# The first key chunk of an adaLN + linear attention + SwiGLU kernel: finer loads, ScalarE normalises, matvecs between the key matmuls

## The chip, the cores and the metric

The kernel runs on one core of a Trainium2 chip. The metric is the device time of one execution in microseconds (us). A profile's span starts at the first instruction, so it is 1.7 to 2.2 us shorter than the time in the runs here.

Engines in the profile: PE is TensorE (matmul), PEld its weight load, DVE is VectorE, ACT is ScalarE, POOL is GpSimd, SPq the queue that issues loads. The granted clock (PEclk) is the share of its full rate that TensorE's clock was given. A matvec is a matmul of a weight block with one column. To modulate a tile is to multiply by `1 + ca` and add `sa`; `xn` is a normalised tile, `tp` its transpose as TensorE writes it, `hT` the copy of `tp` that the matmuls read.

## The reference, cut to what matters

```python
x = A_x                                               # 2048 x 1024, bf16
mod = (silu(c) @ w_mod).reshape(1, 6, 1, -1)          # sa, ca, ga, sb, cb, gb
h = layernorm(x) * (1 + ca) + sa
qkv = h @ wqkv                                        # then linear attention with phi(q), phi(k)
x = x + ga * (attention(qkv) @ wo)
h = layernorm(x) * (1 + cb) + sb
x = x + gb * ((silu(h @ w_gate) * (h @ w_up)) @ w_down)
```

This is about the first 34 us: `layernorm` of the first 512 rows, the modulation vectors `ca` and `sa`, and the first 64 matmuls of `h @ wqkv` for the keys.

## The kernel before

The rows are worked on in four chunks of 512, each of four tiles of 128. In the first chunk everything has to arrive at once. Cut to the opening:

```python
for st in range(STC - 1):                  # three x tiles first; c was issued before them
    load_x(st, nc.sync)
for b in range(2):
    for q in (1, 0):                       # ca block, then sa block, 1 MB each
        t = big("wme", [DC, NB])
        nc.sync.dma_start(out=t[:], in_=wm_v[:, :, q * D + b * NB:...])
    for i in range(2):                     # two key rows of 128 x 1024 in one load
        nc.sync.dma_start(out=wk[b][:, 2 * i:2 * i + 2, :], in_=...)
    if b == 0:
        load_x(STC - 1, nc.sync)
# ... cut ...
def pe_transpose_tile(hT, xn, t):
    tp = acc_b("tp", (DC, P), BF16)
    for cc in range(DC):
        transpose(tp[:, cc, :], xn[:, cc * P:(cc + 1) * P])
    h = DC // 2
    nc.scalar.copy(out=hT[:, 0:h, ...], in_=tp[:, 0:h, :])
    nc.vector.tensor_copy(out=hT[:, h:DC, ...], in_=tp[:, h:DC, :])
# ... cut ...
keep_warm(accs[5], 26)                     # warmers: matmuls whose result is not used
with in_order(nc.vector, nc.scalar, nc.gpsimd):
    st0 = ln1_stats(0, 0)
    st1 = ln1_stats(0, 1)
    xn0 = ln1_norm(*st0)                   # VectorE normalises in chunk 0
    st2 = ln1_stats(0, 2)
    xn1 = ln1_norm(*st1)
    pe_transpose_tile(hTs[0], xn0, 0)
    xn2 = ln1_norm(*st2)
    keep_warm(accs[5], 4)                  # and 4 after tile 1 and after tile 2
    # ... cut ...
    for b in range(2):
        mod_block(b, 1); keep_warm(idle, 2)    # 32 matvecs for ca
        mod_block(b, 0); keep_warm(idle, 3)    # 32 matvecs for sa
        for cc in range(4 * b, 4 * b + 4):
            modulate(hTs[0], cc, ca1T, saT, 0, 3 * P)
        if b == 0:
            xn3 = ln1_norm(*ln1_stats(0, 3))
            k_mms(0, gs, accs, 0, 4)       # 24 key matmuls
            pe_transpose_tile(hTs[0], xn3, 3)
        else:
            k_mms(0, gs, accs, 4, 8)       # 24 more
    # ... cut: modulate tile 3, the last 16 key matmuls, evacuation
build_masks()                              # GpSimd memsets, needed much later
```

`ln1_stats` takes mean and variance on VectorE (`mv`) and the reciprocal root `rstd` on GpSimd. When ScalarE normalises, GpSimd must also compute `nmr = -mean * rstd`. `in_order` pins the traced order of instructions on VectorE, ScalarE and GpSimd; the scheduler may still put other instructions between them.

Of the kernel before, what the change touches and what calls it, by code (L numbers as in the profile page):

```python
# [8 lines left out]
ACT = mybir.ActivationFunctionType  # L9
# [12 lines left out]
def kernel(  # L22
# [13 lines left out]
    nc = tc.nc  # L36
    P = nc.NUM_PARTITIONS
    _, S, D = A_x.shape
# [4 lines left out]
    DC = D // P  # L43
    HG = DC
    FC = F // P
    SCW = 512
    NSC = S // SCW
    STC = SCW // P
    NB = 512
# [11 lines left out]
    wqkv_v = A_wqkv.rearrange("(c p) n -> p c n", p=P)  # L61
# [4 lines left out]
    wm_v = w_mod.rearrange("(p j) n -> p j n", j=DC)  # L66
    c_v = c.rearrange("o (p j) -> p (o j)", j=DC)
# [12 lines left out]
    last_on = {}  # L80

    @contextmanager
    def in_order(*engines):
        types = [e.engine for e in engines]
        traced = nc.cur_bb.bb.instructions
        mark = traced[-1]
        yield
        first = next(k for k in reversed(range(len(traced))) if traced[k] is mark) + 1
        for i in traced[first:]:
            if i.engine in types:  # L90
                prev = last_on.get(i.engine)
                if prev is not None:
                    tc.add_manual_dep(i, prev.name, mybir.DependencyInfo(
                        mybir.DependencyClass.NoSync, mybir.DependencyReason.DATA), reason="in_order")
                last_on[i.engine] = i

    def mm(out, lhsT, rhs, start, stop):
        return tc.keep_in_program_order(nc.tensor.matmul(out, lhsT=lhsT, rhs=rhs, start=start, stop=stop))  # L98

    def transpose(out, in_):  # L100
        return tc.keep_in_program_order(nc.tensor.transpose(out, in_, ident[:]))  # L101

    def big(name, shape):
        return k8.tile([P] + shape, BF16, name=name, tag="k8")
# [4 lines left out]
    def acc_b(name, shape=(NB,), dt=F32):  # L109
        return pb.tile([P] + list(shape), dt, name=name, tag="pb")  # L110
# [1 line left out]
    x1_dram = dram.tile([S, D], F32, name="x1_scratch")  # L112

    c_sb = const.tile([P, DC], BF16, name="c_sb")
    nc.sync.dma_start(out=c_sb[:], in_=c_v)

    x_tiles = {}

    def load_x(st, eng):
        x_sb = k2.tile([P, D], BF16, name="x_sb")  # L120
        eng.dma_start(out=x_sb[:], in_=x2[st * P:(st + 1) * P, :])
        x_tiles[st] = x_sb

    for st in range(STC - 1):
        load_x(st, nc.sync)

    wme = []
    wk = [big("wk", [4, D]), big("wk", [4, D])]
    for b in range(2):
        ts = []  # L130
        for q in (1, 0):
            t = big("wme", [DC, NB])
            nc.sync.dma_start(out=t[:], in_=wm_v[:, :, q * D + b * NB:q * D + (b + 1) * NB])
            ts.append(t)
        wme.append(ts)
        for i in range(2):
            nc.sync.dma_start(out=wk[b][:, 2 * i:2 * i + 2, :], in_=wqkv_v[:, 4 * b + 2 * i:4 * b + 2 * i + 2, D:2 * D])
        if b == 0:
            load_x(STC - 1, nc.sync)

    def load_w(view, lo, name):
        ts = []
# [14 lines left out]
    nc.vector.memset(neg_half[:], -0.5)  # L157

    scT = const.tile([P, DC], BF16, name="scT")
    nc.scalar.activation(out=scT[:], in_=c_sb[:], func=ACT.Silu)  # L160
    sc32 = const.tile([P, DC, 32], BF16, name="sc32")

    saT = const.tile([P, DC], F32, name="saT")
    ca1T = const.tile([P, DC], F32, name="ca1T")
# [37 lines left out]
    def normalise(dst, src, mean, rstd):  # L202
        nc.vector.tensor_scalar(out=dst, in0=src, scalar1=mean, scalar2=rstd, op0=ALU.subtract, op1=ALU.mult)

    def normalise_act(dst, src, mv, rstd):
        nmr = small.tile([P, 1], F32, name="nmr")
        nc.gpsimd.tensor_scalar(out=nmr[:], in0=mv[:, 0, 0:1], scalar1=rstd[:, 0:1], scalar2=-1.0,  # L207
                                op0=ALU.mult, op1=ALU.mult)
        nc.scalar.activation(out=dst, in_=src, func=ACT.Identity, bias=nmr[:], scale=rstd[:, 0:1])  # L209

    def modulate(hT, cc, scaleT, biasT, lo=0, hi=SCW):
        nc.vector.tensor_scalar(out=hT[:, cc, lo:hi], in0=hT[:, cc, lo:hi], scalar1=scaleT[:, cc:cc + 1],  # L212
                                scalar2=biasT[:, cc:cc + 1], op0=ALU.mult, op1=ALU.add)

    def pe_transpose_tile(hT, xn, t):
        tp = acc_b("tp", (DC, P), BF16)
        for cc in range(DC):
            transpose(tp[:, cc, :], xn[:, cc * P:(cc + 1) * P])
        h = DC // 2
        nc.scalar.copy(out=hT[:, 0:h, t * P:(t + 1) * P], in_=tp[:, 0:h, :])  # L220
        nc.vector.tensor_copy(out=hT[:, h:DC, t * P:(t + 1) * P], in_=tp[:, h:DC, :])

    hTs = {}

    def ln1_stats(sc, t):
        x_sb = x_tiles.pop(sc * STC + t)
        mv = small.tile([P, STC, 2], F32, name="mv")
        bn(x_sb, mv[:, 0, :])
        rstd = rstd_of(mv, 1)
        return sc, t, x_sb, mv, rstd  # L230

    def ln1_norm(sc, t, x_sb, mv, rstd):
        xn = k2.tile([P, D], BF16, name="xn", bufs=4)
        if sc == 0:
            normalise(xn[:], x_sb[:], mv[:, 0, 0:1], rstd[:, 0:1])
            return xn
        normalise_act(xn[:], x_sb[:], mv, rstd)
        nc.sync.dma_start_transpose(hTs[sc][:, :, t * P:(t + 1) * P], xn[:])

    def ln1(sc):  # L240
        hTs[sc] = big("hT", [DC, SCW])
        for t in range(STC):
            ln1_norm(*ln1_stats(sc, t))

    def mod_block(b, q):
        k = 1 - q
        for i in range(4):
            col = q * DC + 4 * b + i
            for j in range(DC):
                mm(mod_ps[:, col:col + 1], lhsT=wme[b][k][:, j, i * P:(i + 1) * P],  # L250
                   rhs=scT[:, j:j + 1], start=(j == 0), stop=(j == DC - 1))
        cs = slice(4 * b, 4 * b + 4)
        src = mod_ps[:, q * DC + 4 * b:q * DC + 4 * b + 4]
        if q == 1:
            nc.vector.tensor_scalar_add(out=ca1T[:, cs], in0=src, scalar1=1.0)
        else:
            nc.vector.tensor_copy(out=saT[:, cs], in_=src)
# [12 lines left out]
    k_groups = [(t, nb) for t in range(STC) for nb in range(NNB)]  # L270

    def k_mms(sc, gs, accs, cc_lo=0, cc_hi=DC):
        for cc in range(cc_lo, cc_hi):
            for (t, nb), acc in zip(gs, accs):
                mm(acc[:], lhsT=hTs[sc][:, cc, t * P:(t + 1) * P], rhs=wk[cc // 4][:, cc % 4, nb * NB:(nb + 1) * NB],
                   start=(cc == 0), stop=(cc == DC - 1))

    def k_evac(sc, gs, accs):
        for (t, nb), acc in zip(gs, accs):
            phi_to(pks[sc][:, t, nb * NB:(nb + 1) * NB], acc[:])  # L280
# [118 lines left out]
    def keep_warm(acc, n):  # L399
        for _ in range(n):  # L400
            mm(acc[:], lhsT=sel[:, 0, :], rhs=sel[:], start=True, stop=True)

    gs = k_groups[0:6]
    accs = [acc_a() if i < 4 else acc_b("acc") for i in range(6)]
    keep_warm(accs[5], 26)
    hTs[0] = big("hT", [DC, SCW])
    pks[0] = big("pk", [STC, D])
    with in_order(nc.vector, nc.scalar, nc.gpsimd):
        st0 = ln1_stats(0, 0)
        st1 = ln1_stats(0, 1)  # L410
        xn0 = ln1_norm(*st0)
        st2 = ln1_stats(0, 2)
        xn1 = ln1_norm(*st1)
        pe_transpose_tile(hTs[0], xn0, 0)
        xn2 = ln1_norm(*st2)
        keep_warm(accs[5], 4)
        pe_transpose_tile(hTs[0], xn1, 1)
        keep_warm(accs[5], 4)
        pe_transpose_tile(hTs[0], xn2, 2)
        keep_warm(accs[5], 4)  # L420
        mod_ps = acc_b("mod_ps")
        for b in range(2):
            idle = accs[5] if b == 0 else accs2[0]
            mod_block(b, 1)
            keep_warm(idle, 2)
            mod_block(b, 0)
            keep_warm(idle, 3)
            for cc in range(4 * b, 4 * b + 4):
                modulate(hTs[0], cc, ca1T, saT, 0, 3 * P)
            if b == 0:  # L430
                xn3 = ln1_norm(*ln1_stats(0, 3))
                k_mms(0, gs, accs, 0, 4)
                pe_transpose_tile(hTs[0], xn3, 3)
                accs2 = [acc_b("acc")]
            else:
                k_mms(0, gs, accs, 4, 8)
        for cc in range(DC):
            modulate(hTs[0], cc, ca1T, saT, 3 * P, SCW)
        gs2 = k_groups[6:8]
        accs2.append(acc_b("acc"))  # L440
        k_mms(0, gs2, accs2)
        k_evac(0, gs, accs)
        k_evac(0, gs2, accs2)
    nc.vector.tensor_copy(out=sc32[:], in_=scT[:].unsqueeze(2).to_broadcast([P, DC, 32]))
    build_masks()

    for sc in range(NSC):
# [204 lines left out]
```

## Time and profile before

| | before |
|---|---|
| time, median of the runs beside the changed kernel | 847.84 us |
| TensorE busy share of the span | 99% |
| tile 0 normalised, tile 2 normalised | 7.93 us, 12.07 us |
| first key matmul | 16.30 us |
| first value matmul (all 64 key matmuls done) | 33.92 us |

The first question is where time can be won at all. The page gives the busy time of each engine and the share of each engine in the chain of work that ended last (before):

```profile
PE 838.6 (99%) x4284; PEld 385.7 (46%) x4284; DVE 307.2 (36%) x602; ACT 173.8 (21%) x267; POOL 55.7 (7%) x160
...
PE 98%; DVE 1%; POOL 0%; DMA 0%; issue 0%; ACT 0%; SPq 0%; DVEq 0%; POOLq 0%
```

The kernel is bound by TensorE. What the opening can gain is only the moment from which TensorE runs densely. The timeline of PE (before; start, length, what, count) shows that moment:

```profile
1.21 7.20 PE L98 MATMUL acc<-sel 128*128 128x512 bf16 x26 [1.21 <-DVE sel L397]
8.25 0.61 PE L101 MATMUL tp<-ident,xn 128*128 128x128 bf16 x8
...
12.13 0.62 PE L101 MATMUL tp<-ident,xn 128*128 128x128 bf16 x8 [0.49 <-DVE xn L203]
...
16.30 5.35 PE L98 MATMUL acc<-wk,hT 128*128 128x512 bf16 x24
...
25.27 8.81 PE L98 MATMUL acc<-wk,hT 128*128 128x512 bf16 x40
33.92 13.98 PE L98 MATMUL acc<-wv,hT 128*128 128x512 bf16 x64
```

The warmers (`acc<-sel`) run from 1.21 us (0.43 us apart until 4.15, then 0.21), the transposes of tile 2 at 12.13, the first key matmuls at 16.30, and from 25.27 on there is no gap. Of the 33.92 us, 64 key matmuls at 0.217 us are 13.9 us.

### The profile page before, as it was taken

Reading aid. Unit: us, or ns where it says so; the run is one execution under the profiler, and the core shown is the slowest. Engines: PE = TensorE matmul, PEld = TensorE weight load, DVE = VectorE, ACT = ScalarE, POOL = GpSimd, SP = SyncE. Lnnn points to the kernel's source line nnn. Section 1 sums busy time; section 2 is a strip of 40 time slices with the busy share of each in tenths; the row PEclk is TensorE's granted clock in tenths of the full one; section 3 lists DMA queues with packets and bytes.
Section 4 is the critical chain, followed back from the end, with each engine's and each line's share of the span. In section 5 each row is a group of like instructions: output and inputs, shape, how many; then the busy total and the mean of one; then the engine's idle time right before and its main releaser. Section 6 shows DMA issues by size and latency. Waiting matters only on the chain.

```text
span 846.2 us, 10498 instructions
## 1 busy us (share of the span) xinstructions
PE 838.6 (99%) x4284; PEld 385.7 (46%) x4284; DVE 307.2 (36%) x602; ACT 173.8 (21%) x267; POOL 55.7 (7%) x160
## 2 busy tenths in 40 slices
PE   8999999999999999999999999999999999999997
PEld 4445445544444444444444444444444444444443
DVE  5756464467423325431111344211114431111121
ACT  1455453354311110101111010011110101111000
POOL 2101010012011001100000010000001100000000
PEclk9999999999999999999999999999999999999999
DMA  9893870029976765528434073581604639710011
GB/s 309 301 257 98 243 187 1 1 52 215 348 210 207 214 186 174 181 69 266 146 104 149 19 236 95 159 283 54 199 1 126 185 69 318 240 59 0 19 57 50
DMA packets 125840, 128.74 MB, mean 152 GB/s; under 512 B 33376, under 2 KB 107360, under 8 KB 125280
## 3 DMA queue, kind: packets, MB, share of 16 engines
q1 hardware_dynamic: 122208, 115.36, 46.0%
q0 software_dynamic: 3584, 12.72, 5.0%
q8 instruction: 33, 0.54, 0.3%
q14 instruction: 15, 0.12, 0.0%
HBM read 108.01 MB, written 12.71 MB: 143 GB/s over the span
## 4 chain that ended last, share of the span: by engine, by line
PE 98%; DVE 1%; POOL 0%; DMA 0%; issue 0%; ACT 0%; SPq 0%; DVEq 0%; POOLq 0%
PE acc L98 88%; PE a_ps L98 7%; PE kvp L98 1%; PE modr L98 0%; PE wf L98 0%; DMA x_sb<-in_A_x_dram 0%; DVE stats L199 0%; PE mod_ps L98 0%; PE den L98 0%; POOL zmask L186 0%; PE tp L101 0%; POOL rstd L193 0%; PE bcr L98 0%; DVE e L583 0%; DVE ob L585 0%
## 5 line engine op out<-in xcount | busy, mean ns | idle before, releaser
L98 PE MATMUL acc<-h2T,wgu 128*128 128x512 bf16 x1792 | 387.9, 379 | 0.0
L98 PEld LDWEIGHTS <-wgu 128*128 128x128 bf16 x1792 | 175.1, 98 | 211.0
L98 PE MATMUL acc<-wd,gu 128*128 128x512 bf16 x896 | 196.0, 379 | 0.0
L566 DVE TENSOR_TENSOR gu<-acc,e 128x512 bf16<-128x512 f32 x112 | 77.4, 691 | 300.4 <-PE acc L98 300.4
L565 ACT ACTIVATE e<-acc 128x512 f32<-128x512 f32 x112 | 66.9, 597 | 375.2 <-PE acc L98 375.2
L98 PEld LDWEIGHTS <-gu 128*128 128x128 bf16 x896 | 87.6, 98 | 105.8
L98 PEld LDWEIGHTS <-hT 128*128 128x128 bf16 x512 | 49.6, 98 | 60.8 <-DVE hT L212 1.0
L583 DVE TENSOR_TENSOR e<-acc,gb_bc 128x512 f32<-128x512 f32 x32 | 22.1, 691 | 130.5 <-PE acc L98 130.5
L98 PE MATMUL a_ps<-wo,pq 128*128 128x512 bf16 x256 | 57.9, 379 | 0.6 <-DVE pq L395 0.6
L98 PE MATMUL acc<-hT,wq 128*128 128x512 bf16 x256 | 57.1, 379 | 0.0
L98 PE MATMUL acc<-wk,hT 128*128 128x512 bf16 x256 | 56.9, 379 | 0.0
L98 PE MATMUL acc<-wv,hT 128*128 128x512 bf16 x256 | 55.9, 379 | 0.0
L263 ACT ACTIVATE eb<-acc 128x512 bf16<-128x512 f32 x64 | 37.9, 596 | 62.8 <-PE acc L98 60.5
L209 ACT ACTIVATE xn<-x,nmr,rstd 128x1024 bf16<-128x1024 f32 x16 | 19.8, 1240 | 127.6 <-POOL nmr L207 127.6
L264 DVE TENSOR_SCALAR eb<-eb 128x512 bf16<-128x512 bf16 x64 | 18.4, 291 | 60.6 <-ACT eb L263 60.6
L98 PEld LDWEIGHTS <-pq 128*128 128x128 bf16 x256 | 24.7, 98 | 31.8 <-DVE pq L395 2.6
L98 PEld LDWEIGHTS <-wq 128*128 128x128 bf16 x256 | 24.9, 98 | 29.8
L534 POOL DMA_DIRECT2D x_scratch<-x x16 | 9.6, 600 | 369.6 <-DVE x L527 369.6
L527 DVE TENSOR_TENSOR x<-a_ps,x_sb 128x512 f32<-128x512 f32 x32 | 22.1, 691 | 8.0 <-PE a_ps L98 7.9
L193 POOL TENSOR_TENSOR rstd<-veps,neg_half 128x1 f32<-128x1 f32 x32 | 18.2, 569 | 81.3 <-DVE veps L191 70.4
L301 ACT CAST v<-acc 128x512 bf16<-128x512 f32 x32 | 18.3, 582 | 22.1 <-PE acc L98 22.1
L528 DVE BATCH_NORM_STATS2 stats<-x 128x6 f32<-128x512 f32 x32 | 22.2, 695 | 1.1
(72 smaller groups left out, 280.7 us busy)
## 6 DMA issues: line engine op xcount, KB each, us to landing
wgu<-in_B_w_gate_dram SPq DMA_DIRECT2D x28, 1024.0 KB, 7.4
wgu<-in_B_w_up_dram SPq DMA_DIRECT2D x28, 1024.0 KB, 8.7
x_sb<-in_A_x_dram SPq DMA_DIRECT2D x32, 256.0 KB, 5.9
wml<-in_w_mod_dram SPq DMA_DIRECT2D x8, 1024.0 KB, 8.6
x_scratch<-x POOLq DMA_DIRECT2D x16, 512.0 KB, 3.1
x1r<-x_scratch SPq DMA_DIRECT2D x32, 256.0 KB, 3.0
wd<-in_B_w_down_dram SPq DMA_DIRECT2D x7, 1024.0 KB, 7.7
wme<-in_w_mod_dram SPq DMA_DIRECT2D x4, 1024.0 KB, 11.2
```

The source lines that it names most:

```text
L98: return tc.keep_in_program_order(nc.tensor.matmul(out, lhsT=lhsT, rhs=rhs, start=start, stop=stop))
L193: nc.gpsimd.tensor_tensor(out=rstd[:, 0:n], in0=veps[:, 0:n], in1=neg_half[:].to_broadcast([P, n]), op=ALU.pow)
L209: nc.scalar.activation(out=dst, in_=src, func=ACT.Identity, bias=nmr[:], scale=rstd[:, 0:1])
L263: nc.scalar.activation(out=e[:], in_=acc, func=ACT.Exp)
L264: nc.vector.tensor_scalar(out=e[:], in0=e[:], scalar1=1.0, scalar2=PHI_EPS, op0=ALU.min, op1=ALU.add)
L301: nc.scalar.copy(out=v[:, t, nb * 4:(nb + 1) * 4, 0:P], in_=acc[:].rearrange("p (g e) -> p g e", e=P))
L527: nc.vector.tensor_tensor(out=x1[:, ns], in0=a_ps[:], in1=x_t[:, ns], op=ALU.add)
L528: nc.vector.bn_stats(out=stats[:, nb, :], in_=x1[:, ns])
L534: nc.gpsimd.dma_start(out=x1_dram[st * P:(st + 1) * P, :], in_=x1[:])
L565: nc.scalar.activation(out=sg[:], in_=ps[0][:], func=ACT.Silu)
L566: gm = nc.vector.tensor_tensor(out=guT[sc][f // GPT][:, f % GPT, :], in0=ps[1][:], in1=sg[:], op=ALU.mult)
L583: nc.vector.tensor_tensor(out=yt[:], in0=y_ps[:], in1=gb_bc[:, ns], op=ALU.mult)
```

## The change

The intent is to pace the first key chunk by its data: load x before c, load key rows in eight pieces between modulation blocks of which one is halved, let ScalarE normalise the first three tiles while VectorE does statistics, drop most of the warmers after the opening ones (22 become 5), and put the matvecs of the second modulation half between key matmuls, with a seventh group of key matmuls started early. The diff, cut to its core (the loads, and `mod_block` taking a range of columns, are shortened):

```diff
-    nc.sync.dma_start(out=c_sb[:], in_=c_v)            # c first
     for st in range(STC - 1):
         load_x(st, nc.sync)
+    nc.sync.dma_start(out=c_sb[:], in_=c_v)            # now after three x tiles
+    load_mod(0, 1, 0, NB)
+    load_mod(0, 0, 0, NB)
+    load_k(0); load_k(1)
+    load_x(STC - 1, nc.sync)
+    load_k(2); load_k(3)
+    load_mod(1, 1, 0, NB)
+    load_mod(1, 0, 0, NB // 2)
+    load_k(4); load_k(5)
+    load_mod(1, 0, NB // 2, NB)
+    load_k(6); load_k(7)
...
-    keep_warm(accs[5], 26)
+    keep_warm(spare, 25)
     with in_order(nc.vector, nc.scalar, nc.gpsimd):
-        # statistics and VectorE's normalise in turn, 4 warmers after each tile
+        st = [ln1_stats(0, t) for t in range(3)]
+        xns = [ln1_norm(*st[t]) for t in range(3)]     # on ScalarE
+        pe_transpose_tile(hT, xns[0], 0, DC)           # VectorE copies all of it
+        keep_warm(spare, 1)
+        mod_block(0, 1, 0, 4)
+        pe_transpose_tile(hT, xns[1], 1, DC)
+        keep_warm(spare, 2)
+        pe_transpose_tile(hT, xns[2], 2, DC // 2)
+        keep_warm(spare, 2)
+        mod_block(0, 0, 0, 2)                          # then modulate 0, 1
+        mod_block(0, 0, 2, 4)                          # then modulate 2, 3
+        k_mms(0, gs, accs, 0, 3)
+        xn3 = ln1_norm(*ln1_stats(0, 3), dve=True)
+        pe_transpose_tile(hT, xn3, 3, DC // 2)
+        k_mms(0, gs, accs, 3, 4)                       # then modulate tile 3
+        mod_block(1, 1, 0, 4)
+        k_mms(0, gs7, accs7, 0, 4)
+        mod_block(1, 0, 0, 2)                          # then modulate 4, 5
+        k_mms(0, gs + gs7, accs + accs7, 4, 5)
+        k_mms(0, gs[0:4], accs[0:4], 5, 6)
+        mod_block(1, 0, 2, 4)                          # then modulate 6, 7
+        k_mms(0, gs[4:6] + gs7, accs[4:6] + accs7, 5, 6)
+        k_mms(0, gs + gs7, accs + accs7, 6, 8)
+        k_mms(0, gs8, accs8)
```

More of the change, by code (lines that the diff above doesn't have):

```diff
@@ L125, with load_mod, load_k @@
         load_x(st, nc.sync)
-    wme = []
+    nc.sync.dma_start(out=c_sb[:], in_=c_v)
     wk = [big("wk", [4, D]), big("wk", [4, D])]
-    for b in range(2):
-        ts = []
-        for q in (1, 0):
-            t = big("wme", [DC, NB])
-            nc.sync.dma_start(out=t[:], in_=wm_v[:, :, q * D + b * NB:q * D + (b + 1) * NB])
-            ts.append(t)
-        wme.append(ts)
-        for i in range(2):
-            nc.sync.dma_start(out=wk[b][:, 2 * i:2 * i + 2, :], in_=wqkv_v[:, 4 * b + 2 * i:4 * b + 2 * i + 2, D:2 * D])
-        if b == 0:
-            load_x(STC - 1, nc.sync)
+    wme = [[big("wme", [DC, NB]) for _ in range(2)] for _ in range(2)]
+    def load_mod(b, q, lo, hi):
+        nc.sync.dma_start(out=wme[b][q][:, :, lo:hi], in_=wm_v[:, :, q * D + b * NB + lo:q * D + b * NB + hi])
+    def load_k(cc):
+        nc.sync.dma_start(out=wk[cc // 4][:, cc % 4, :], in_=wqkv_v[:, cc, D:2 * D])
+    load_mod(0, 1, 0, NB)
+    load_mod(0, 0, 0, NB)
+    load_k(0)
+    load_k(1)
+    load_x(STC - 1, nc.sync)
+    load_k(2)
+    load_k(3)
+    load_mod(1, 1, 0, NB)
+    load_mod(1, 0, 0, NB // 2)
+    load_k(4)
+    load_k(5)
+    load_mod(1, 0, NB // 2, NB)
+    load_k(6)
+    load_k(7)
     def load_w(view, lo, name):
@@ L159 @@
     scT = const.tile([P, DC], BF16, name="scT")
-    nc.scalar.activation(out=scT[:], in_=c_sb[:], func=ACT.Silu)
     sc32 = const.tile([P, DC, 32], BF16, name="sc32")
@@ L213, in modulate, with pe_transpose_tile @@
                                 scalar2=biasT[:, cc:cc + 1], op0=ALU.mult, op1=ALU.add)
-    def pe_transpose_tile(hT, xn, t):
+    def pe_transpose_tile(hT, xn, t, split):
         tp = acc_b("tp", (DC, P), BF16)
@@ L218, in pe_transpose_tile @@
             transpose(tp[:, cc, :], xn[:, cc * P:(cc + 1) * P])
-        h = DC // 2
-        nc.scalar.copy(out=hT[:, 0:h, t * P:(t + 1) * P], in_=tp[:, 0:h, :])
-        nc.vector.tensor_copy(out=hT[:, h:DC, t * P:(t + 1) * P], in_=tp[:, h:DC, :])
+        if split < DC:
+            nc.scalar.copy(out=hT[:, split:DC, t * P:(t + 1) * P], in_=tp[:, split:DC, :])
+        nc.vector.tensor_copy(out=hT[:, 0:split, t * P:(t + 1) * P], in_=tp[:, 0:split, :])
     hTs = {}
@@ L230, in ln1_stats, with ln1_norm @@
         return sc, t, x_sb, mv, rstd
-    def ln1_norm(sc, t, x_sb, mv, rstd):
+    def ln1_norm(sc, t, x_sb, mv, rstd, dve=False):
         xn = k2.tile([P, D], BF16, name="xn", bufs=4)
-        if sc == 0:
+        if dve:
             normalise(xn[:], x_sb[:], mv[:, 0, 0:1], rstd[:, 0:1])
-            return xn
-        normalise_act(xn[:], x_sb[:], mv, rstd)
-        nc.sync.dma_start_transpose(hTs[sc][:, :, t * P:(t + 1) * P], xn[:])
+        else:
+            normalise_act(xn[:], x_sb[:], mv, rstd)
+        if sc > 0:
+            nc.sync.dma_start_transpose(hTs[sc][:, :, t * P:(t + 1) * P], xn[:])
+        return xn
     def ln1(sc):
@@ L243, in ln1, with mod_block @@
             ln1_norm(*ln1_stats(sc, t))
-    def mod_block(b, q):
-        k = 1 - q
-        for i in range(4):
+    def mod_block(b, q, lo, hi):
+        for i in range(lo, hi):
             col = q * DC + 4 * b + i
             for j in range(DC):
-                mm(mod_ps[:, col:col + 1], lhsT=wme[b][k][:, j, i * P:(i + 1) * P],
+                mm(mod_ps[:, col:col + 1], lhsT=wme[b][q][:, j, i * P:(i + 1) * P],
                    rhs=scT[:, j:j + 1], start=(j == 0), stop=(j == DC - 1))
-        cs = slice(4 * b, 4 * b + 4)
-        src = mod_ps[:, q * DC + 4 * b:q * DC + 4 * b + 4]
+        cs = slice(4 * b + lo, 4 * b + hi)
+        src = mod_ps[:, q * DC + 4 * b + lo:q * DC + 4 * b + hi]
         if q == 1:
@@ L404 @@
     accs = [acc_a() if i < 4 else acc_b("acc") for i in range(6)]
-    keep_warm(accs[5], 26)
-    hTs[0] = big("hT", [DC, SCW])
+    spare = accs[5]
+    keep_warm(spare, 25)
+    hT = hTs[0] = big("hT", [DC, SCW])
     pks[0] = big("pk", [STC, D])
+    H = 3 * P
     with in_order(nc.vector, nc.scalar, nc.gpsimd):
-        st0 = ln1_stats(0, 0)
-        st1 = ln1_stats(0, 1)
-        xn0 = ln1_norm(*st0)
-        st2 = ln1_stats(0, 2)
-        xn1 = ln1_norm(*st1)
-        pe_transpose_tile(hTs[0], xn0, 0)
-        xn2 = ln1_norm(*st2)
-        keep_warm(accs[5], 4)
-        pe_transpose_tile(hTs[0], xn1, 1)
-        keep_warm(accs[5], 4)
-        pe_transpose_tile(hTs[0], xn2, 2)
-        keep_warm(accs[5], 4)
-        mod_ps = acc_b("mod_ps")
-        for b in range(2):
-            idle = accs[5] if b == 0 else accs2[0]
-            mod_block(b, 1)
-            keep_warm(idle, 2)
-            mod_block(b, 0)
-            keep_warm(idle, 3)
-            for cc in range(4 * b, 4 * b + 4):
-                modulate(hTs[0], cc, ca1T, saT, 0, 3 * P)
-            if b == 0:
-                xn3 = ln1_norm(*ln1_stats(0, 3))
-                k_mms(0, gs, accs, 0, 4)
-                pe_transpose_tile(hTs[0], xn3, 3)
-                accs2 = [acc_b("acc")]
-            else:
-                k_mms(0, gs, accs, 4, 8)
-        for cc in range(DC):
-            modulate(hTs[0], cc, ca1T, saT, 3 * P, SCW)
-        gs2 = k_groups[6:8]
-        accs2.append(acc_b("acc"))
-        k_mms(0, gs2, accs2)
@@ new lines @@
+        nc.scalar.activation(out=scT[:], in_=c_sb[:], func=ACT.Silu)
+        st = [ln1_stats(0, t) for t in range(3)]
+        xns = [ln1_norm(*st[t]) for t in range(3)]
+        mod_ps = acc_b("mod_ps")
+        pe_transpose_tile(hT, xns[0], 0, DC)
[6 more added lines that the diff above has]
+        mod_block(0, 0, 0, 2)
+        for cc in (0, 1):
+            modulate(hT, cc, ca1T, saT, 0, H)
@@ new lines @@
+        mod_block(0, 0, 2, 4)
+        for cc in (2, 3):
+            modulate(hT, cc, ca1T, saT, 0, H)
+        k_mms(0, gs, accs, 0, 3)
+        xn3 = ln1_norm(*ln1_stats(0, 3), dve=True)
+        pe_transpose_tile(hT, xn3, 3, DC // 2)
+        k_mms(0, gs, accs, 3, 4)
+        for cc in range(4):
+            modulate(hT, cc, ca1T, saT, H, SCW)
+        mod_block(1, 1, 0, 4)
+        gs7, accs7 = k_groups[6:7], [acc_b("acc")]
+        k_mms(0, gs7, accs7, 0, 4)
+        mod_block(1, 0, 0, 2)
@@ L442 @@
+        for cc in (4, 5):
+            modulate(hT, cc, ca1T, saT)
+        k_mms(0, gs + gs7, accs + accs7, 4, 5)
+        k_mms(0, gs[0:4], accs[0:4], 5, 6)
+        mod_block(1, 0, 2, 4)
+        for cc in (6, 7):
+            modulate(hT, cc, ca1T, saT)
+        k_mms(0, gs[4:6] + gs7, accs[4:6] + accs7, 5, 6)
+        k_mms(0, gs + gs7, accs + accs7, 6, 8)
+        gs8, accs8 = k_groups[7:8], [acc_b("acc")]
+        k_mms(0, gs8, accs8)
         k_evac(0, gs, accs)
-        k_evac(0, gs2, accs2)
@@ L444 @@
-    nc.vector.tensor_copy(out=sc32[:], in_=scT[:].unsqueeze(2).to_broadcast([P, DC, 32]))
+        k_evac(0, gs7, accs7)
+        k_evac(0, gs8, accs8)
+    with tc.issue_after(last_on[nc.vector.engine]):
+        nc.vector.tensor_copy(out=sc32[:], in_=scT[:].unsqueeze(2).to_broadcast([P, DC, 32]))
     build_masks()
```

## The prediction

> **What bounds the kernel now.** The profile's busy table gives TensorE 99% of the 846.2 us span, and the chain of waits is 98% TensorE. From the first value matmul at 33.92 us (timeline) it runs without gaps, and the change leaves that part alone: the instruction orders differ only in the opening. So the stake is only when that first value matmul starts. The opening holds 64 key matmuls at 0.217 us (24 took 5.35 us less pipeline tail), 13.9 us; everything else is waiting. The most that perfect pacing could give is far below 2% (17 us).
>
> **Opening before (timeline).** Row tiles land from 4.04; VectorE does statistics and normalises, xn done at 7.9, 10.1, 12.07; transposes of tile 2 at 12.13; modulation matvecs and warmers; first key matmul 16.30. Then 17.6 us to 33.92: 13.9 key matmuls, 0.45 transposes, 1.6 matvecs (32 in 0.80), about 1.6 warmers and waits. DMA does not bind: the last key rows land at 25.7, used after 27.9.
>
> **What the change does.**
> 1. c is issued after x: x lands 0.4 us earlier (about 3.6).
> 2. ScalarE normalises at 1.24 us a tile against 0.55 on VectorE. In GpSimd's new order all three rstd precede the first nmr. Three statistics periods of 1.63 end at 8.6, rstd 2 at 9.2, a mask memset 0.3, nmr 9.9: xn0 done about 11.1, xn1 12.4, xn2 13.7, which is 1.6 us later than now.
> 3. The transposes share the single free PSUM buffer: tile 2's first transpose waits for VectorE's copy of tile 1 (0.7 us estimated for 1024 columns from 0.42 for 512). Tile 2 transposes at about 14.1.
> 4. One modulation block moves into the gaps, and some warmers go. From tile 2's transposes to the first key matmul 2.4 us instead of 4.2. The copies of tile 2 remain serial (ScalarE 0.58, then VectorE 0.42), then saT and modulate. First key matmul about 16.5, no gain.
> 5. Afterwards warmers (1.4 us) vanish, but new waits appear: tile 3's statistics come after four modulates and only 18 key matmuls cover them (wait about 0.4); the matvec pair for row 4 uncovered, saT plus modulate (about 0.85, as 15.48 to 16.29 before); row 6 about 0.2. Value start about 33.9.
> 6. Finer loads: same bytes in the same order, DMA still saturated, landing within 1 us of now, before use. [...]
>
> So gain and loss nearly cancel: predicted first value matmul 32.5 to 35.5, centre 33.8, and 847.6 us, range 846.2 to 849.2.
>
> **Risk.** TensorE idles from about 8.0 (25 warmers) to 11.2, some 3.2 us. [...] matmuls 0.427 us apart until 4.15, then 0.21. A cold restart would put transposes and matvecs at double spacing, about 1 to 1.5 us more (chance a fifth).
>
> **What would show it.** xn0 done near 11.1 on ScalarE; a TensorE gap of 3 us from 8.0; first key matmul near 16.5; waits of TensorE on hT before rows 4 and at tile 3's transposes; no DMA release of TensorE after 10 us; granted clock at 11 to 14 us.
>
> **What would make it wrong.** x landing earlier or the scheduler's rstd order not costing as computed (faster by 1 to 2 us); cold clock, or late key rows (slower).
>
> Chances: faster by over 2% 0.01, within 2% 0.98, slower 0.01.

Where a cut is marked, a passage was taken out because no trace or run shows what it said: one in step 6, one in the risk. Neither was a term of the forecast's sum: step 6 called its passage off the chain, and the risk stood beside the sum as a chance. So the sum is whole as it stands, 33.8 us for the first value matmul and 847.6 us for the time. That TensorE's idling could halve the clock at all was the author's assumption. The 1 to 1.5 us are an estimate from the spacings of the opening warmers, 0.427 and 0.21 us in the trace before.

## More of the kernel before

All runs told of here were classed as fast by their time. Inside that class the mean clock granted to TensorE still ranges from 0.996 to 1.000, and this turns out to matter, so it is given beside the times.

## The result, and the profile after

The changed kernel took 847.75 us in the median of four runs, before 847.84 in four. The ratio is 0.9992 with a 95% interval of 0.9978 to 1.0007, so the same. (Ratios here are the mean time of one kernel's fast runs over that of the other's of the same rounds, so not quite the ratio of the medians quoted.) The four runs are not alike: 847.67, 847.84 and 847.99 us had a granted clock of 0.997, and 846.54 us had 0.999 (no trace of that one was kept).

The PE timeline after (same columns; the profiled run is the one of 847.84 us):

```profile
1.21 7.65 PE L98 MATMUL acc<-sel 128*128 128x512 bf16 x25 [1.21 <-DVE sel L407]
10.87 0.62 PE L101 MATMUL tp<-ident,xn 128*128 128x128 bf16 x8 [2.01 <-ACT xn L218]
...
13.16 1.06 PE L98 MATMUL acc<-sel 128*128 128x512 bf16 x2
14.01 1.06 PE L101 MATMUL tp<-ident,xn 128*128 128x128 bf16 x8
14.87 1.01 PE L98 MATMUL acc<-sel 128*128 128x512 bf16 x2
...
17.01 4.06 PE L98 MATMUL acc<-wk,hT 128*128 128x512 bf16 x18
...
25.65 2.55 PE L98 MATMUL acc<-wk,hT 128*128 128x512 bf16 x11 [0.70 <-DVE hT L221]
...
34.04 13.98 PE L98 MATMUL acc<-wv,hT 128*128 128x512 bf16 x64
```

The reader should see three things. The first transposes wait 2.01 us for ScalarE. The second and third group of eight transposes and the warmers beside them are slow (eight transposes took 0.62 us at 10.87 and 1.06 at 14.01). And the first key matmul came 0.71 us later than before, the first value matmul 0.12 us later: from first key to first value matmul the new placement took 17.03 us (34.04 - 17.01) against 17.62 (33.92 - 16.30). A loss of 0.7 in the first part ate a gain of 0.6 in the second.

Why the transposes are slow is in the table of stretches (after; stretch, length, busy time of PE, PEld, DVE, ACT, POOL with counts, granted clock, DMA share, GB/s):

```profile
5.46:8.87 3.41, 3.40 (x16) 1.37 (x14) 2.81 (x8) 0.14 (x1) 1.27 (x3) 1.00 1.05 360
8.87:12.28 3.41, 1.42 (x39) 1.30 (x40) 0.69 (x1) 2.71 (x3) 2.84 (x41) 1.00 1.07 367
12.28:15.69 3.41, 3.41 (x28) 2.34 (x26) 0.85 (x2) 1.38 (x2) 0.00 (x0) 0.50 1.06 371
```

The clock was exactly half (0.50) for the 3.41 us after a stretch of equal length in which TensorE was busy for 1.42 us. Before, no such stretch was so empty (2.92 us busy at least), and the table shows a clock of 1.00 through the opening (before; same columns):

```profile
7.56:10.97 3.41, 2.98 (x26) 1.69 (x25) 2.79 (x7) 0.75 (x2) 3.07 (x39) 1.00 1.07 360
10.97:14.38 3.41, 2.92 (x49) 1.85 (x47) 1.31 (x3) 1.01 (x2) 0.52 (x1) 1.00 1.05 381
```

Why ScalarE's tile was late is in the timeline of POOL and ACT. First before, where VectorE needs only `rstd`:

```profile
5.93 0.55 POOL L193 TENSOR_TENSOR rstd<-veps,neg_half 128x1 f32<-128x1 f32 x1 [4.53 <-DVE veps L191]
7.55 0.79 POOL L193 TENSOR_TENSOR rstd<-veps,neg_half 128x1 f32<-128x1 f32 x1 [1.07 <-DVE veps L191]
...
9.15 1.70 POOL L186 MEMSET zmask<- 32x1 bf16 x32
...
10.94 0.55 POOL L193 TENSOR_TENSOR rstd<-veps,neg_half 128x1 f32<-128x1 f32 x1
```

and after:

```profile
5.24 0.55 POOL L202 TENSOR_TENSOR rstd<-veps,neg_half 128x1 f32<-128x1 f32 x1 [3.85 <-DVE veps L200]
...
8.48 0.55 POOL L202 TENSOR_TENSOR rstd<-veps,neg_half 128x1 f32<-128x1 f32 x1 [1.07 <-DVE veps L200]
8.98 0.31 POOL L190 MEMSET zmask<- 128x256 bf16 x1
9.27 0.73 POOL L216 TENSOR_SCALAR nmr<-mv,rstd 128x1 f32<-128x1 f32 x3
9.57 3.50 ACT L218 ACTIVATE xn<-x_sb,nmr,rstd 128x1024 bf16<-128x1024 bf16 x3 [3.97 <-POOL nmr L216]
```

The first `rstd` was done at 5.79 us, but its `nmr` was queued behind the `rstd` of tiles 1 and 2 and a memset, and started at 9.27: 3.5 us between ready and start. In this trace GpSimd did not take the ready `nmr` ahead of them; `in_order` had pinned the three `rstd` in front of it.

### The profile page after: what moved, and what is told of

The parts are those of the page before. It is cut to its first block, busy times and chain, and to the rows that moved or that the text cites. A ratio compares the mean times of both kernels' runs of the same rounds, so it can differ in the third digit from the quotient of the medians.

```text
span 846.1 us, 10472 instructions
## 1 busy us (share of the span) xinstructions
PE 837.1 (99%) x4266; PEld 385.0 (46%) x4266; DVE 306.4 (36%) x597; ACT 176.0 (21%) x268; POOL 55.6 (7%) x163
## 4 chain that ended last, share of the span: by engine, by line
PE 98%; DVE 1%; DMA 0%; ACT 0%; issue 0%; POOL 0%; DVEq 0%
PE acc L98 88%; PE a_ps L98 7%; PE kvp L98 1%; DVE stats L208 0%; PE modr L98 0%; PE wf L98 0%; PE tp L101 0%; PE mod_ps L98 0%; DMA x_sb<-in_A_x_dram 0%; PE den L98 0%; ACT xn L218 0%; PE bcr L98 0%; DVE e L602 0%; DVE pq L405 0%; DVE ob L604 0%
```

## The experiments

Theory: the placement and the missing warmers do gain, and this is hidden by the late `nmr`, which delays the tiles and, by leaving TensorE idle, halves the clock for 3.41 us. Rival A: only the clock matters, the order on GpSimd does not. Rival B: the chunk is paced by the loads, so neither matters, or the finer loads are what helps or hurts. All kernels below gave correct results. By the rule of 2% each of them counts as the same as before; the intervals show differences of tenths of a per cent.

### More opening warmers

```diff
-    keep_warm(spare, 25)
+    keep_warm(spare, 36)
```

> The changed kernel with 36 instead of 25 opening warmers, so that TensorE is busy until ScalarE's first normalised tile at 10.8 us. Theory (three things hide each other: the late normalise, the clock drop it causes, the warmers saved): the halved clock from 12.3 to 15.7 us goes away, first value matmul about 32.8 instead of 34.04 us, time 846.5 us as in the one of four runs of the changed kernel that showed clock 0.999, and every run so. Rival (the clock drop is hidden behind other waits): first value matmul within 0.3 us of 34.04 and 847.7 us.

Measured: 846.9 us (846.24 to 847.6), clock 1.000 in all five runs; ratio to before 0.9987 (0.9974 to 0.9999). The clock drop is gone in every run, as the theory said. The time fell less than it said, because in the profiled run the 36 warmers overran: the first transposes started at 11.57, when tile 0 had been ready since about 10.9. So the size was measured again:

```diff
-    keep_warm(spare, 25)
+    keep_warm(spare, 30)
```

> The changed kernel with 30 opening warmers: TensorE's gap before tile 0 shrinks from 2 us to about 1 us and the warmers no longer overrun the normalised tile as 36 did. Theory (the clock drop costs 1.3 us): clock at least 0.999, 846.5 us. Rival (the gap is not what drops the clock): clock 0.997 and 847.9 us as the changed kernel.

Measured: 846.55 us (846.29 to 846.76), clock 0.999 or 1.000 in all five; ratio 0.9978 (0.9966 to 0.999). PE timeline of this run (up to 40 us, where the last line is cut off):

```profile
1.21 8.03 PE L98 MATMUL acc<-sel 128*128 128x512 bf16 x30 [1.21 <-DVE sel L407]
10.85 0.62 PE L101 MATMUL tp<-ident,xn 128*128 128x128 bf16 x8 [1.61 <-ACT xn L218]
...
13.20 0.61 PE L101 MATMUL tp<-ident,xn 128*128 128x128 bf16 x8
...
15.42 4.06 PE L98 MATMUL acc<-wk,hT 128*128 128x512 bf16 x18
...
32.47 7.72 PE L98 MATMUL acc<-wv,hT 128*128 128x512 bf16 x35
```

Tile 0 is transposed at the same moment as in the changed kernel (10.85 against 10.87), yet the first key matmul is 1.59 us earlier and the first value matmul 1.57 us. So the halved clock cost the changed kernel 1.6 us, and five more matmuls that compute nothing win it back. What the runs don't settle is how much idling it takes: 1.61 us of gap kept the clock here, 2.01 us lost it there, but the two runs also differ in when the opening warmers became dense (by their weight loads at 5.45 us in the changed kernel and at 4.11 here), and whether that matters was not shown.

### The order on GpSimd

```diff
-        st = [ln1_stats(0, t) for t in range(3)]
-        xns = [ln1_norm(*st[t]) for t in range(3)]
+        xns = [ln1_norm(*ln1_stats(0, t)) for t in range(3)]
```

> The changed kernel with each tile's normalise traced right behind its statistics, so that GpSimd computes nmr of tile 0 before rstd of tiles 1 and 2. Theory: xn of tile 0 about 7.4 instead of 10.8, tile 2 about 12.1 (mask memsets sit before nmr 2) instead of 13.1, no TensorE gap of 2 us, clock full, first key matmul about 14.6 instead of 17.0, first value matmul about 31.6, time about 845.4 us. Rival A (only the clock counts): 846.5. Rival B (the finer loads pace the chunk): 847.7.

Measured: 845.43 us (845.11 to 845.95), clock 0.999 or 1.000; ratio 0.9971 (0.9958 to 0.9983). GpSimd and ScalarE in this run:

```profile
5.22 0.55 POOL L202 TENSOR_TENSOR rstd<-veps,neg_half 128x1 f32<-128x1 f32 x1 [3.82 <-DVE veps L200]
5.72 0.31 POOL L190 MEMSET zmask<- 128x256 bf16 x1
6.01 0.26 POOL L216 TENSOR_SCALAR nmr<-mv,rstd 128x1 f32<-128x1 f32 x1
6.31 1.24 ACT L218 ACTIVATE xn<-x_sb,nmr,rstd 128x1024 bf16<-128x1024 bf16 x1 [0.42 <-POOL nmr L216]
```

Tile 0 was normalised at 7.55 instead of 10.82 us, the first key matmul came at 14.33 and the first value matmul at 31.37. This is better than repairing the clock alone (32.47), so rival A falls. In this profile the first transposes (9.22) followed the warmers and no longer tile 0, and the matvecs (9.88) started as the first modulation block landed (their weight loads had waited 0.17 us for it): warmers and loads now set the start. One change of trace order moved the first value matmul 2.67 us forward (34.04 - 31.37). Repeated:

> The run that only reorders GpSimd, again beside the other kernels of this batch: 845.4 us, clock at least 0.999 in all runs, and faster than before with an interval clear of 1. Rival (its first result was luck of the clock): some runs at 847 us or more with clock 0.998.

Measured: 845.53 us in the median of six, ratio 0.997 (0.9959 to 0.9982). Five runs lay between 845.2 and 845.98 with a clock of at least 0.999, one took 847.7 with 0.998. So the gain holds, but the expectation of a full clock in every run does not.

### VectorE normalises after all

```diff
-        xns = [ln1_norm(*st[t]) for t in range(3)]
+        # order of before: stats 0, stats 1, norm 0, stats 2, norm 1, norm 2
+        xns = [ln1_norm(*st0, dve=True), ...]
```

> The changed kernel, but VectorE normalises the first three tiles in the order of before (0.55 us a tile), everything else as changed. Theory (it was the order on GpSimd, not ScalarE as such, that made the normalise late): xn of tile 0 about 6.9, tile 2 about 11.5 us because the mask memsets sit before rstd 2 as in the kernel before; first value matmul about 31, time 845.3 us, level with the run that only reordered GpSimd. Rival (taking the normalise off VectorE is what helps): slower than 846.5 us.

Measured: 845.6 us in the median of six, ratio 0.9979 (0.9966 to 0.9992). Four runs lay between 845.22 and 845.62 with a clock of at least 0.999, two at 848.1 and 848.4 with 0.998. In the profile tile 0 was done at 7.34 us, tile 2 at 11.21, and the first value matmul came at 31.12. With a full clock this equals the reordered kernel with ScalarE. So it did not matter which engine normalises; it mattered that tile 0 is not held back.

### The loads

The loads as before, in the changed kernel:

```diff
-    load_k(0); load_k(1)     # ... eight loads of one key row, one modulation block halved
+    load_k2(0); load_k2(2)   # four loads of two key rows, whole modulation blocks
```

> The changed kernel with the loads as before (four loads of two key rows, whole modulation blocks), x still before c. Theory: no load is waited for in the changed kernel after 10 us, so the time stays 847.7 us within 0.3 (or 846.5 where the clock happens to stay full). Rival B (finer loads matter): slower by over 1 us.

Measured: 848.08 us (848.01 to 848.29), clock 0.997 in all five; ratio 1.0001 (0.9988 to 1.0013). The waits of PE contain no DMA at all, as in the changed kernel, and the first value matmul is at 33.92. The finer loads are worth nothing there, and rival B falls for the changed kernel. Then with the chain shortened, first the masks of GpSimd moved away:

```diff
         k_evac(0, gs8, accs8)
+        build_masks()            # inside in_order: behind the chunk's own GpSimd work
```

> As the second run, and the mask memsets of GpSimd moved behind the first key chunk. Theory: xn of tile 2 about 10.7 us, first key matmul about 13.8, first value matmul about 30.8, time about 844.6 us, with the last modulation block and key rows landing at 24 to 25 us just ahead of their use. Rival B (loads pace the chunk): no better than the second run. Rival A (only the clock counts): 846.5.

Measured: 845.92 us (844.71 to 846.72), ratio 0.9975 (0.9961 to 0.9988): not better than the reorder alone. The waits of PE in this run (engine, line, waited for, us in total, times, longest) say why:

```profile
PE acc L98 <- DVE sel L407: 1.2, 1, 1.2
PE mod_ps L98 <- DMA wme<-in_w_mod_dram: 0.9, 2, 0.7
PE acc L98 <- DVE hT L221: 0.7, 1, 0.7
```

Tile 2 is no longer waited for (0.36 us in the run with the reorder alone), but it was transposed at 11.93 instead of 12.09, because the matvecs in front of it now waited for the first modulation blocks to land, at about 10.2 and 13.1 us. The first value matmul came at 31.51, not at 30.8. Here the loads do bind, so the theory's figure of 844.6 was too low (one run of five, 844.71, came near it). And the coarse loads in this version:

> The reordered kernel with masks moved (845.9 us in the first batch), with the loads as before. Theory: now the chunk runs close to the loads, the last whole modulation block lands about 23 us where its first half is wanted at 21.8, so about 1 us slower, 846.7 us, with a DMA release of TensorE between 21 and 24 us. Rival (the finer loads are worth nothing here either): 845.9 us.

Measured: 846.05 us (845.38 to 848.34), ratio 0.9982 (0.997 to 0.9995). The three runs with a full clock took 845.38, 845.56 and 846.05; the kernel with fine loads had 844.71 to 846.12 in its four with at least 0.999. No difference is resolved, so the expected 1 us is not seen. The two other runs took 847.95 and 848.34 with 0.998, and the profile is of the latter. It shows waits for loads (1.1 us for a modulation block, 0.8 us for key rows, and 1.15 us for tile 3, whose x these loads put behind four key rows, the fine ones behind two) and, after them, the clock at half in the middle of the key matmuls (table of stretches of this run, columns as above):

```profile
20.98:24.39 3.41, 2.56 (x54) 1.75 (x53) 2.06 (x9) 0.87 (x1) 0.41 (x5) 1.00 1.05 384
24.39:27.80 3.41, 3.41 (x9) 1.22 (x8) 0.01 (x1) 0.00 (x0) 0.00 (x0) 0.50 1.05 386
```

In the second stretch only 9 matmuls ran, about 0.43 us apart. Whether coarse loads make this drop likelier is open: two of five runs here and one of five with fine loads is too few.

### The kernel before, with its masks moved

In the kernel before, the same memsets hold back the `rstd` of tile 2 (its input was ready at 9.55, it started at 10.94). The edit is that of the masks shown above.

> The kernel before with only the mask memsets of GpSimd moved behind the first key chunk. Theory: rstd of tile 2 starts about 9.6 instead of 10.94, tile 2 transposes about 11 instead of 12.1, the modulation matvecs then wait for the second modulation block landing at about 13.5; first key matmul about 15.2 to 15.4 instead of 16.3, time 846.9 us. Rival (the opening of before is bound by loads): 847.9 us.

Measured: 848.11 us (847.29 to 849.75), ratio 1.0005 (0.9992 to 1.0018). A miss. In its profile tile 2 is no longer waited for, but it was transposed at 11.96, against 12.13 before, and directly behind warmers: here the 26 opening warmers lasted 8.29 us instead of 7.20, and the fixed number of warmers between the tiles used the rest. In this profile what GpSimd gained was hidden by TensorE's own queue of warmers. In the profile of the kernel before TensorE did wait 0.49 us for tile 2, so up to about that may be won where the opening warmers end early; these runs don't resolve it.

### Only the later placement

```diff
 # before, up to its first key matmul and with its loads; then as changed:
-            k_mms(0, gs, accs, 0, 4)      # and matvec blocks with 5 warmers
+        k_mms(0, gs, accs, 0, 3)          # seven groups, matvecs between them, no warmers
```

> The kernel before up to its first key matmul and with its loads, then the changed placement: seven groups, matvecs between key matmuls, no warmers. Theory: the placement alone saves about 0.6 us (17.6 to 17.0 us from first key to first value matmul), so 847.3 us where before is 847.9; tile 3 waits and the wait before row 4 appear as in the changed kernel. Rival (the placement saves its 1.4 us of warmers in full): 846.5 us.

Measured: 847.79 us (847.54 to 847.85), clock at least 0.999; ratio 0.9992 (0.9979 to 1.0005). From first key to first value matmul it took 16.94 us (33.02 - 16.08) against 17.62, so the placement saves 0.7 us in the chunk. The time fell by 0.4 us in the medians (848.17 beside it), within the scatter. (From the first value matmul to the end of the span the profiles took 811.9 to 812.7 us, so a gain of a few tenths in the opening is not told by a time.) The rival's full 1.4 us did not come, because the wait before row 4 is there (0.70 us for hT).

### Covering the remaining waits

Built on the reorder with masks moved: VectorE alone copies tiles 2 and 3, a fourth key row runs before tile 3's transposes, and the matvecs for rows 4 and 5 come before the seventh group's four matmuls, which are to cover the modulate.

> The reordered kernel with masks moved, plus: VectorE alone copies tiles 2 and 3 (0.7 us instead of 0.58 and then 0.43), row 3 of the key matmuls before tile 3's transposes, the matvecs for rows 4 and 5 before the seventh group's four key matmuls, so that they cover saT and modulate. Theory (the remaining TensorE waits of 0.7, 0.4 and 0.2 us on hT are real cost): first value matmul about 30.5 instead of 31.4, time about 844.5 us, and the wait of TensorE on hT before row 4 under 0.3 us. Rival (loads now bind): no faster than 845.4 us, with DMA releases of TensorE.

Measured: 846.77 us (845.22 to 848.36), ratio 0.9981 (0.9969 to 0.9994), three of five runs with a clock of 0.998 or less. The two full-clock runs (845.22, 845.33) were no faster than the reorder. The wait on hT is gone, but a new one stands in its place in the waits of PE:

```profile
PE mod_ps L98 <- DVE ca1T L265: 1.1, 1, 1.1
```

All matvecs write one accumulator, `mod_ps`. The matvecs for `sa` now followed at once and had to wait until VectorE had read `ca` from it, and VectorE was busy modulating tile 3. Reading first mends it:

```diff
-        for cc in range(4):
-            modulate(hT, cc, ca1T, saT, H, SCW)
         mod_block(1, 1, 0, 4)             # its last step reads ca1T
+        for cc in range(4):
+            modulate(hT, cc, ca1T, saT, H, SCW)
         mod_block(1, 0, 0, 2)
```

> The previous cover run with ca1T taken before the modulates of tile 3, so that the matvecs for rows 4 and 5 no longer wait 1.09 us for VectorE to have read the shared accumulator. Theory: first value matmul about 30.5 (31.2 before the fix), 844.6 us in runs with full clock; runs in which the clock drops inside the chunk stay 1.5 to 3 us slower, so the median may be higher. Rival (the shared accumulator wait is hidden): 845.3 us in its full-clock runs.

Measured: 844.77 us in the median of six, ratio 0.9965 (0.995 to 0.9979). Four runs lay between 844.35 and 844.94, one at 846.05, one at 847.92 with a clock of 0.998. The first value matmul is at 30.37, and the waits of PE are:

```profile
PE mod_ps L98 <- DMA wme<-in_w_mod_dram: 0.8, 2, 0.6
PE mod_ps L98 <- DVE saT L267: 0.3, 1, 0.3
```

This is the best version, 0.35% faster than the kernel before. The changed kernel was not run beside it; its own ratio to before was 0.9992. Of the waits that are left after the first warmer, most are for loads.

## Why the prediction was right or wrong

The number was right: 847.6 us predicted, 847.75 measured, and the forecast that gain and loss nearly cancel held (first value matmul forecast at 33.8, seen at 34.04). But the sum reached it with two errors of opposite sign, and that they cancelled was luck.

1. *x lands 0.4 us earlier.* Forecast 3.6 us, seen 3.44 (4.06 before), so 0.6 us earlier. Right.
2. *All three rstd before the first nmr.* Right, and the cause of the loss: the first `nmr` was forecast ready at 9.9, and ScalarE had it at 9.57; tile 0 done 11.1 and 10.82; tile 2 done 13.7 and 13.07. "1.6 us later than now" was really 1.0 us (13.07 - 12.07). This term was mis-sized: ScalarE started 0.33 us earlier than forecast, and its three tiles took 3.50 us instead of the 3.8 that the forecast allowed (13.7 - 9.9). That undoing this order alone moves the first value matmul from 34.04 to 31.37 and the ratio from 0.9992 to 0.9971 confirms the cause; the regained clock is 1.57 us of that (the run with 30 warmers), the earlier tiles the other 1.10.
3. *"Tile 2's first transpose waits for VectorE's copy of tile 1."* This step failed. The changed kernel's profile seems to bear it out (14.1 forecast, 14.01 seen), but there the halved clock did it: the two warmers before it were issued 0.43 us apart, and the transposes even began before the copy (13.40 to 14.09) had ended. With a full clock (30 warmers) the transposes of tile 2 start at 13.20, while VectorE copies tile 1 from 12.97 to 13.66:

```profile
12.97 0.69 DVE L230 COPY hT<-tp 128x1024 bf16<-128x1024 bf16 x1 [0.31 <-PE tp L101]
13.20 0.61 PE L101 MATMUL tp<-ident,xn 128*128 128x128 bf16 x8
```

   So at least two buffers were free, and the transposes followed only the tile (done at 13.05) and the warmers in front of them. The forecast had allowed 0.4 us for this wait (14.1 - 13.7); 0.15 us was seen (13.20 - 13.05).
4. *First key matmul about 16.5, no gain.* With a full clock it is 15.42, a gain of 0.9 us over before. In the profiled run it was 17.01. Both sides of the forecast are wrong, by 1.1 and 0.5 us.
5. *New waits later.* The wait before row 4 was forecast at 0.85 and measured 0.70. Tile 3's transposes were to wait 0.4; the last of the 18 key matmuls was issued at about 20.7 (17.01 + 17 x 0.217), so by about 20.9 TensorE was free, and the transposes came at 20.99: some 0.1 us. The part was forecast at 17.4 us (16.5 to 33.9) and took 17.03.
6. *Loads never bind.* Right for the changed kernel, though "in the same order" was not exact (tile 3's x now comes before two key rows): no DMA among the waits of PE, and coarse loads give the same time. It was right only as long as the chain was long; in the shortened versions loads do bind, for 0.8 to 0.9 us.
7. *Risk: cold clock, chance a fifth, 1 to 1.5 us.* The clock did halve, at about the forecast size (1.6 us); the chance was wrong: by their mean clock of 0.997 three of four runs, and five of five with coarse loads, had it. The chance of a fifth was my estimate, and it rested on nothing that a trace made before shows. I computed 3.2 us of gap; the gap was 2.01 us and the clock dropped all the same.

So for a full clock the forecast of the opening was about 1.4 us too slow (first value matmul 33.9 forecast, 32.47 with 30 warmers). Of this, 1.1 us lies before the first key matmul: about 0.65 in step 2 (tile 2 done at 13.05 with 30 warmers, not at 13.7), 0.25 in step 3, 0.2 in step 4 (2.22 us from the transposes to the first key matmul, not 2.4). Without these errors the forecast would have been near 846.2 (847.6 - 1.4); the lucky run took 846.54 and the 30-warmer kernel 846.55. The halved clock, held unlikely, then took 1.6 us back.

## What to carry to other kernels

When a list of stages is traced stage by stage (all statistics, then all normalises), look at the small steps between them (`rstd` and `nmr` on GpSimd here): with the order pinned as here that became "the first tile waits for the last" (3.5 us from ready to start), and interleaving the two in the trace cost nothing here. Filler matmuls are part of the schedule: too many of them eat the gain of a shorter chain (36 of them ran past the moment at which tile 0 was ready, by 0.6 us), and with too few the clock was halved after a gap (25 of them, a gap of 2.01 us, 1.6 us lost here; with 30, a gap of 1.61 us, it was not). And before trusting that a forecast moment was hit for the forecast reason, look at a run in which the suspected cause is absent.

## What the traces show of the clock, and what they leave open

- In the changed kernel the clock was 0.50 from 12.28 to 15.69 us, after 3.41 us in which TensorE was busy for 1.42 us, with one gap of 2.01 us. In the profile with coarse loads and the reorder it was 0.50 from 24.39 to 27.80 us, after 3.41 us in which the profile counts TensorE busy for 2.56. The busy time that the profile counts does not tell the two cases apart: with 30 warmers TensorE was busy for 1.80 of the 3.41 us from 8.87, and the clock was 1.00 there and in the next 3.41 us. In the stretch with 2.56 us 48 of the 54 matmuls were matvecs; whether that matters, no run here shows.
- The time of the same 25 opening warmers differs from profile to profile: 7.65 us in the changed kernel's, 8.17 in the reordered one, and from 6.88 to 8.53 in the others. The time of the reordered kernel also differs by about 2 us between its runs with a clock of at least 0.999 (845.2 to 845.98 us) and the one with 0.998 (847.7). Only one run with a clock of 0.998 has a trace, the one with coarse loads and the reorder, and there the clock halved in the middle of the key matmuls.
